# One mask product over two PSUM banks, and the old state added on the PE

## The chip, the cores and the metric

The kernel runs on 1 core of one Trainium2 chip. The metric is the device time in microseconds of a whole execution. PE is TensorE (products), PEld its weight load, DVE VectorE, ACT ScalarE, POOL GpSimd, SP SyncE, which issues most DMAs.

## The reference, cut to what matters

```
for t in range(S):                      # B=4, H=8, S=768, D=48
    state = alpha[:, :, t, :, None] * state + einsum('bhd,bhe->bhde', k[:, :, t], v[:, :, t])
    y[:, :, t] = einsum('bhd,bhde->bhe', q[:, :, t], state)
x = y as (3072 rows, 384)
# first MoE: each row goes to the one of 8 experts with the largest logit
out[mask] = gate_w[mask, None] * (maximum(x[mask] @ w1[e], 0) @ w2[e])      # F=1024
# second MoE: every row through 4 experts, weighted by domain_probs
out += p[:, e:e + 1] * (maximum(x @ w1[e], 0) @ w2[e])
```

## The kernel before, in words

`tile_main` (L40) opens the pools and calls `attention_and_routing` (L339) and `experts` (L114). Instructions run on each engine in the order in which the program writes them; a library places the semaphore waits, from the tiles that instructions read and write. Two PSUM pools serve the whole first part: `psA` with two buffers of one bank each (L98), which take turns, and `ps1` with six single ones.

**Attention, 24 units of 128 time steps.** A sequence has six units (index `u`, `c = u % 6`). The decay is folded into q and k: `prep1` (L421) makes two running products with DVE scans (`G` L434, `bf` L446), `prep2` multiplies them onto k and q, mostly on POOL (L459, L460). One unit is spread over three turns of the loop at L819:

- `S1(u)` (L473): 8 score products (L480) go alternately to two tiles `A` of `psA`, one per half of the heads, 4 x 128 columns each; two DVE products with the triangle mask `tri` (L485) bring them to SBUF as `At`, one per half. Four transposes `kn` (L492) follow.
- `S3(u)` (L554): `fin` (L558) turns the finished rows, ACT copies them out.
- `S2(u)` (L506): `y` from `At` and v (L516) and, if `c > 0`, from the old state `S` and q (L525); the new part of the state goes to the PSUM tile `U` (L537, if `c < 5`). `state()` (L543) is put at the end of the turn: on DVE, for `c = 0`, `S = U * bcall` (L547); for `c` from 1 to 4 first `U = U + S_old` (L549) and then `S = U * bcall` (L550).

Turn `i` calls `S1(i)`, `S3(i-2)`, `S2(i-1)`, so the PE does A(i), kn(i), fin(i-2), y(i-1), U(i-1), and the DVE does bf scans, At(i), routing steps, G scans, state(i-1). A(i+1) cannot start until At(i) has read the tiles `A`. Every six units a group of rows is routed, scaled and scattered by POOL (L653).

**Early rows.** The first 224 rows of the first expert window are worked while routing ends. `early_rows` (L681) transposes them into two `psA` tiles `ext`, one for two column blocks, one for the third; `cut` copies each out (ACT L675, then the remainder on DVE L676). `early_g1` (L694) makes the hidden layer for a pair of 128-blocks in one `psA` tile `eh`; `early_relu` (L707) takes it out on ACT (L710) and DVE (L711); `early_g2` (L715) adds up `eo`. The DVE part of `early_relu(0)` is written after the routing steps of the last group, behind the products of the second pair.

**First expert.** In `experts`, `xpose(0)` (L179) turns the other 224 rows in three steps (`xt` L192, ACT `xh` L197, DVE `xl` L198), each in the next `psA` tile. For each of 8 blocks `f`, `gemm1` (L132, products L135 to L137) fills a `psA` tile `h`, `h_split` (L123) takes it out on ACT (`hh` L126) and DVE (`hl` L127), and `g2(f-1)` (L224, products L233 to L235) follows, so that the products of `f` and of `f-1` alternate. At L247 these pools are closed. From the second expert on, and in the second MoE (L322), other PSUM pools are used.

Of the kernel before, what the change touches and what calls it, by code (L numbers as in the profile page):

```python
# [7 lines left out]
F32 = mybir.dt.float32  # L8
# [5 lines left out]
ALU = mybir.AluOpType  # L14
AX = mybir.AxisListType
PSUM = bass.MemoryType.PSUM

B, H, S, D = 4, 8, 768, 48
# [12 lines left out]
R = 112  # L31
# [7 lines left out]
@with_exitstack  # L39
def tile_main(ctx: ExitStack, tc: tile.TileContext, a: dict, out: bass.AP):  # L40
    nc = tc.nc

    const = ctx.enter_context(tc.tile_pool(name="const", bufs=1))
    small = ctx.enter_context(tc.tile_pool(name="small", bufs=2))
    dram = ctx.enter_context(tc.tile_pool(name="dram", bufs=1, space=bass.MemoryType.DRAM))

    xs = dram.tile([E1 * NR, DM], F32, name="xs")
    info_d = dram.tile([NT, 8], F32, name="info_d")


    units = [(0, e, f) for e in range(E1) for f in range(NFB)]
    units += [(1, e, f) for e in range(E2) for f in range(NFB)]
    wraw, wtile, ids = {}, {}, {}
    w_loaded, w_split = [0], [0]

    def load_w(n):
        while w_loaded[0] < min(n, len(units)):
            u = w_loaded[0]
            t = wst.tile([128, 2 * DM], F32, tag="wraw", name="wraw")
            src = a["wu"][u]  # L60
            if NFB <= u < E1 * NFB:
                e = a["wu"][0:E1 * NFB].rearrange("(e f) r c -> e f r c", f=NFB)
                src = e[bass.ds(ids[u // NFB], 1), u % NFB].rearrange("o r c -> (o r) c")
            nc.sync.dma_start(out=t, in_=src)
            wraw[u] = t
            w_loaded[0] += 1

    def split_w(n):
        while w_split[0] < min(n, len(units)):
            u = w_split[0]  # L70
            load_w(u + 1)
            r = wraw.pop(u)
            t = wun.tile([128, 2, 2 * DM], F32R, tag="wu", name="wu")
            nc.scalar.activation(out=t[:, 0], in_=r, func=AF.Copy)  # L74
            nc.gpsimd.tensor_tensor(out=t[:, 1], in0=r, in1=t[:, 0].bitcast(F32), op=ALU.subtract)  # L75
            wtile[u] = t
            w_split[0] += 1

    with tc.manual_schedule():
        ti = const.tile([128, 2, 128], F32, name="ti")  # L80
        ident = ti[:, 1]
        inf = const.tile([128, 24, 8], F32, name="inf")
        keep = {
            "ident": ident,
            "ti": ti,
            "ordi": const.tile([128, 8], I32, name="ordi"),
            "offi": const.tile([128, 8], I32, name="offi"),
            "posi": const.tile([128, 24], I32, name="posi"),
            "inf": inf,
            "flag": const.tile([1, 1], I32, name="flag"),  # L90
            "ft": const.tile([128, 3], F32, name="ft"),
            "ones": const.tile([128, 8], F32, name="ones"),
        }
        with ExitStack() as fast:
            wun = fast.enter_context(tc.tile_pool(name="wun", bufs=10))
            wst = fast.enter_context(tc.tile_pool(name="wst", bufs=3))
            banks = fast.enter_context(ExitStack())
            ps = (banks.enter_context(tc.tile_pool(name="psA", bufs=2, space=PSUM)),  # L98
                  banks.enter_context(tc.tile_pool(name="ps1", bufs=1, space=PSUM)))
            scat = attention_and_routing(tc, a, small, keep, xs, info_d, wst, wtile, load_w, split_w, *ps)  # L100
            experts(fast, tc, a, keep, small, xs, info_d, scat, wtile, ids, load_w, split_w, out, banks, *ps)

    bad = nc.values_load(keep["flag"][0:1, 0:1], min_val=0, max_val=1000)
    with tc.If(bad > 0):
        general(tc, a, ident, out)


def order(tc, ins, names, why):
# [230 lines left out]
def attention_and_routing(tc, a, small, keep, xs, info_d, wst, wtile, load_w, split_w, psA, ps1):  # L339
    nc = tc.nc  # L340
    ident = keep["ident"]
# [3 lines left out]
    with ExitStack() as ctx:  # L345
# [14 lines left out]
        tri = keep["ti"][:, 0]  # L360
# [4 lines left out]
        Sb = [c1.tile([R, 4, D], F32, name=f"S{j}") for j in range(2)]  # L365
# [107 lines left out]
        def S1(u):  # L473
            g, cl = divmod(u, 3)
            At = wk.tile([128, 2, 4, 128], F32, tag="At", name="At")
            ps = [psA.tile([128, 4, 128], F32, tag="A", name=f"A{h}") for h in range(2)]
            for p in range(4):
                kt, qq = (x[g, p // 2][:, 2 * cl + p % 2, :] for x in (kts, qqs))
                for h in range(2):
                    nc.tensor.matmul(  # L480
                        ps[h][:, p, :], lhsT=kt[64 * h:64 * h + D], rhs=qq[64 * h:64 * h + D],
                        start=(p == 0), stop=True, skip_group_check=True,
                    )
            for h in range(2):
                nc.vector.tensor_tensor(  # L485
                    out=At[:, h], in0=ps[h], in1=tri.unsqueeze(1).to_broadcast([128, 4, 128]), op=ALU.mult
                )
            Ats[u] = At
            if u % 6 < 5:
                pk = ps1.tile([128, 4, R], F32, tag="kn", name="kn")  # L490
                for p in range(4):
                    nc.tensor.matmul(  # L492
                        pk[:, p, :], lhsT=kts[g, p // 2][:, 2 * cl + p % 2, :], rhs=ident[0:R, 0:R],
                        is_transpose=True, start=(p == 0), stop=True, skip_group_check=True,
                    )
                kn = wk.tile([128, 4, R], F32, tag="kn", name="kn_s")
                nc.scalar.activation(out=kn, in_=pk, func=AF.Copy)
                kns[u] = kn
# [7 lines left out]
        def S2(u):  # L506
            g, cl = divmod(u, 3)
            c = u % 6
            At, v = Ats.pop(u), vins[g]
            py = ps1.tile([112, 4, 128], F32, tag="y", name="y")  # L510
            for p in range(4):
                for s in range(2):
                    o = py[0:64, p, :] if s == 0 else py[64:112, p, :]
                    c0 = p * 96 + s * 48
                    n = 64 if s == 0 else 48
                    nc.tensor.matmul(  # L516
                        o, lhsT=v[:, cl, c0:c0 + n], rhs=At[:, s, p, :],
                        start=(p == 0), stop=(c == 0), skip_group_check=True,
                    )
            if c:  # L520
                st = Sb[u % 2]
                for p in range(4):
                    qq = qqs[g, p // 2][:, 2 * cl + p % 2, :]
                    for h in (slice(0, D), slice(64, 64 + D)):
                        nc.tensor.matmul(  # L525
                            py[h, p, :], lhsT=st[h, p], rhs=qq[h], start=False, stop=True, skip_group_check=True
                        )
            yt = wk.tile([112, 4, 128], F32, tag="yt", name="yt")
            nc.scalar.activation(out=yt, in_=py, func=AF.Copy)
            yts[u] = yt  # L530
            if c < 5:
                kn = kns.pop(u)
                pu = ps1.tile([R, 4, D], F32, tag="U", name="U")
                for p in range(4):
                    for h in (slice(0, 64), slice(64, R)):
                        c0 = p * 96 + h.start // 64 * D
                        nc.tensor.matmul(  # L537
                            pu[h, p, :], lhsT=kn[:, p, h], rhs=v[:, cl, c0:c0 + D],
                            start=(p == 0), stop=True, skip_group_check=True,
                        )  # L540
                g2, cl2 = divmod(u + 1, 3)

                def state():  # L543
                    sn, so = (Sb[(u + j) % 2] for j in (1, 0))
                    bcv = bcall[:, g2, cl2].unsqueeze(2).to_broadcast([R, 4, D])
                    if c == 0:
                        nc.vector.tensor_tensor(out=sn, in0=pu, in1=bcv, op=ALU.mult)  # L547
                    else:
                        nc.vector.tensor_tensor(out=pu, in0=pu, in1=so, op=ALU.add)  # L549
                        nc.vector.tensor_tensor(out=sn, in0=pu, in1=bcv, op=ALU.mult)  # L550

                late.append(state)

# [265 lines left out]
        for i in range(NU + 5):  # L819
# [26 lines left out]
            if 0 < i < NU:  # L846
                S1(i)
# [7 lines left out]
            if 0 <= i - 1 < NU:  # L855
                S2(i - 1)
# [62 lines left out]
        def dot(out, t, x):  # L919
# [32 lines left out]
            out=pv, in0=ohb, in1=off.unsqueeze(1).to_broadcast([128, NU, 8]), op=ALU.mult  # L952
# [341 lines left out]
```

## Time and profile before

| | |
|---|---|
| three runs | 1221.97, 1223.74, 1224.63 us; median 1223.74 us |
| profiled execution | 1219.32 us, its span 1217.5 us |
| mean granted clock of the PE | 0.987 |
| busy: PE, DVE, ACT, POOL | 1177.6, 393.9, 326.5, 306.8 us |
| chain that ended last | PE 87%, DVE 4%, issue 3% |

The span runs from the first to the last instruction of the profiled execution; 1.8 us of its time lie around it. A row of the timeline gives the start, the duration, the engine, the line, out<-in, how many instructions are merged, and in brackets how long the engine had been idle and what ended that.

### The profile page before, as it was taken

What the parts mean: (1) busy time and instruction counts of PE and PEld (TensorE: products, weight loads), DVE (VectorE), ACT (ScalarE), POOL (GpSimd) and SP (SyncE); (2) the same over time, 40 slices, a digit from 0 to 9 for tenths busy, and PEclk for the clock granted to TensorE, in tenths of its full rate; (3) what the DMA queues carried; (4) which work ended last, traced back from release to release, by engine and by line L of the source; (5) the groups of instructions that cost most, each with busy time, mean ns of one, the idle gap of its engine ahead of it and who ended that gap; (6) DMA issues with size and microseconds to landing.
All of it is one profiled execution on the core that took longest, in us unless ns stands there. A gap on an engine that the chain in (4) does not pass through costs nothing.

```text
span 1217.5 us, 17436 instructions
## 1 busy us (share of the span) xinstructions
PE 1177.6 (97%) x7219; PEld 1078.6 (89%) x7219; DVE 393.9 (32%) x823; ACT 326.5 (27%) x640; POOL 306.8 (25%) x221
## 2 busy tenths in 40 slices
PE   5999979999999999999999999999999999999996
PEld 4788879999999999999999999999999999999996
DVE  8989553222222222222212222222222122222221
ACT  3466534444444311111311111221111131111111
POOL 3567543766666300000400000130000030111111
PEclk9999989999999999999999999999999999999998
DMA  9995125544443300000300000120000010000000
GB/s 236 298 278 174 54 100 172 155 141 140 133 123 121 81 1 1 1 1 1 90 15 1 1 1 1 30 75 1 1 1 1 1 40 1 27 27 26 26 27 29
DMA packets 30032, 79.98 MB, mean 66 GB/s; under 512 B 7352, under 2 KB 11064, under 8 KB 28376
## 3 DMA queue, kind: packets, MB, share of 16 engines
q1 hardware_dynamic: 26104, 69.25, 19.5%
q0 software_dynamic: 3840, 9.54, 2.2%
q8 instruction: 58, 0.95, 0.3%
q14 instruction: 30, 0.25, 0.1%
HBM read 65.21 MB, written 13.57 MB: 65 GB/s over the span
## 4 chain that ended last, share of the span: by engine, by line
PE 87%; DVE 4%; issue 3%; ACT 0%; POOL 0%; DVEq 0%; POOLq 0%; ACTq 0%
PE h L135 14%; PE h L137 13%; PE h L136 13%; PE p L303 11%; PE p L302 11%; PE p L301 10%; PE o L234 3%; PE o L235 3%; PE o L233 3%; PE fin L558 1%; PE y L516 1%; PE A L480 1%; DVE bf L446 1%; DVE G L434 1%; DVE At L485 1%
## 5 line engine op out<-in xcount | busy, mean ns | idle before, releaser
L127 DVE SCALAR_TENSOR_TENSOR hl<-h,hh 128x512 fp32r<-128x512 f32 (+9 forms) x264 | 169.9, 644 | 733.4 <-ACT hh L126 719.0
L126 ACT ACTIVATE hh<-h 128x512 fp32r<-128x512 f32 (+9 forms) x264 | 148.2, 562 | 727.1 <-PE h L137 725.3
L75 POOL TENSOR_TENSOR wu<-wraw,wu 128x768 fp32r<-128x768 f32 x96 | 176.6, 1841 | 643.9 <-ACT wu L74 643.7
L303 PE MATMUL p<-wu,hl 128*128 128x384 f32 x768 | 258.8, 337 | 0.0
L302 PE MATMUL p<-wu,hh 128*128 128x384 f32 x768 | 258.2, 336 | 0.0
L301 PE MATMUL p<-wu,hh 128*128 128x384 f32 x768 | 258.0, 336 | 0.0
L135 PE MATMUL h<-x,wu 128*128 128x512 f32 (+1 forms) x600 | 233.0, 388 | 0.0
L137 PE MATMUL h<-x,wu 128*128 128x512 f32 (+1 forms) x600 | 230.6, 384 | 0.0
L136 PE MATMUL h<-x,wu 128*128 128x512 f32 (+1 forms) x600 | 227.9, 380 | 0.0
L302 PEld LDWEIGHTS p<-wu,hh 128*128 128x128 f32 x768 | 144.3, 188 | 7.4
L301 PEld LDWEIGHTS p<-wu,hh 128*128 128x128 f32 x768 | 144.4, 188 | 7.1
L303 PEld LDWEIGHTS p<-wu,hl 128*128 128x128 f32 x768 | 144.3, 188 | 0.0
L137 PEld LDWEIGHTS h<-x,wu 128*128 128x128 f32 x600 | 112.6, 188 | 26.6
L136 PEld LDWEIGHTS h<-x,wu 128*128 128x128 f32 x600 | 112.8, 188 | 16.1
L135 PEld LDWEIGHTS h<-x,wu 128*128 128x128 f32 x600 | 112.8, 188 | 14.5
L74 ACT ACTIVATE wu<-wraw 128x768 fp32r<-128x768 f32 x96 | 80.4, 840 | 39.6 <-PE p L303 34.1
L314 POOL DMA_INDIRECT out_dram<-acc,toki x24 | 23.4, 975 | 183.4 <-DVE acc L310 178.5
L135 PE MATMUL h<-xh,wu 128*128 128x224 f32 (+7 forms) x192 | 67.4, 351 | 0.3 <-DVE xl L198 0.3
L234 PE MATMUL o<-hl,wu 128*128 128x224 f32 (+7 forms) x192 | 65.6, 341 | 0.1
L233 PE MATMUL o<-hh,wu 128*128 128x224 f32 (+7 forms) x192 | 65.6, 342 | 0.0
L136 PE MATMUL h<-xh,wu 128*128 128x224 f32 (+7 forms) x192 | 65.5, 341 | 0.0
L137 PE MATMUL h<-xl,wu 128*128 128x224 f32 (+7 forms) x192 | 65.5, 341 | 0.0
(164 smaller groups left out, 1086.2 us busy)
## 6 DMA issues: line engine op xcount, KB each, us to landing
wraw<-in_wu_dram SPq DMA_DIRECT2D x96, 384.0 KB, 3.1
tin<-in_aqk_dram SPq DMA_DIRECT2D x14, 1011.1 KB, 11.4
xw<-xs SPq DMA_DIRECT2D x7, 672.0 KB, 6.6
v<-in_v_dram SPq DMA_DIRECT2D x8, 576.0 KB, 10.3
xs<-pre SPq DMA_DIRECT2D x8, 480.0 KB, 11.0
tin<-in_aqk_dram SPq DMA_DIRECT2D x2, 448.0 KB
tin<-in_aqk_dram SPq DMA_DIRECT2D x2, 225.8 KB, 4.4
tin<-in_aqk_dram SPq DMA_DIRECT2D x2, 224.0 KB
```

What stands on the lines that cost most here:

```text
L74: nc.scalar.activation(out=t[:, 0], in_=r, func=AF.Copy)
L75: nc.gpsimd.tensor_tensor(out=t[:, 1], in0=r, in1=t[:, 0].bitcast(F32), op=ALU.subtract)
L126: nc.scalar.activation(out=hh[:, 0:n], in_=ps, func=AF.Relu)
L127: nc.vector.scalar_tensor_tensor(out=hl[:, 0:n], in0=ps, scalar=0.0, in1=hh[:, 0:n].bitcast(F32), op0=ALU.max, op1=ALU.subtract)
L135: nc.tensor.matmul(ps, lhsT=w[:, 0, ks], rhs=xh(k), start=(k == 0), stop=False)
L136: nc.tensor.matmul(ps, lhsT=w[:, 1, ks], rhs=xh(k), start=False, stop=False)
L137: nc.tensor.matmul(ps, lhsT=w[:, 0, ks], rhs=xl(k), start=False, stop=(k == KD - 1))
L233: nc.tensor.matmul(o, lhsT=w[:, 0, ds], rhs=hh[:, 0:n], start=(f == 0), stop=False)
L234: nc.tensor.matmul(o, lhsT=w[:, 0, ds], rhs=hl[:, 0:n], start=False, stop=False)
L301: nc.tensor.matmul(o, lhsT=hh[:, js], rhs=w[:, 0, DM:2 * DM], start=(f == 0), stop=False)
L302: nc.tensor.matmul(o, lhsT=hh[:, js], rhs=w[:, 1, DM:2 * DM], start=False, stop=False)
L303: nc.tensor.matmul(o, lhsT=hl[:, js], rhs=w[:, 0, DM:2 * DM], start=False, stop=(f == NFB - 1))
```

## The change

`psA` becomes one tile `A` of two banks (512 columns each), in a class `Banks` that hands out the halves in turn. `S1` writes both halves as before, and one DVE instruction over 1024 columns masks both. For `c` from 1 to 4 the PE adds the old state to `U` with a product of the identity (112 x 112) and `S` (112 x 192), and the DVE addition L549 is gone. Everything else that used `psA` (`ext`, `eh`, `xt` of the first expert, `h` of the first expert) now writes halves of the tile `A`.

```diff
-            ps = (banks.enter_context(tc.tile_pool(name="psA", bufs=2, space=PSUM)),
+            ps = (Banks(banks.enter_context(tc.tile_pool(name="psA", bufs=1, space=PSUM))),
...
+class Banks:
+    def __init__(self, pool):
+        self.both = pool.tile([128, 2, 512], F32, name="A")
+        self.n = 0
+    def tile(self, shape, *_, **__):
+        self.n += 1
+        return self.both[0:shape[0], self.n % 2, 0:shape[1]]
...
-            ps = [psA.tile([128, 4, 128], F32, tag="A", name=f"A{h}") for h in range(2)]
+            ps = psA.both.rearrange("p h (a c) -> p h a c", a=4)
...
-            for h in range(2):
-                nc.vector.tensor_tensor(
-                    out=At[:, h], in0=ps[h], in1=tri.unsqueeze(1).to_broadcast([128, 4, 128]), op=ALU.mult
-                )
+            nc.vector.tensor_tensor(
+                out=At.rearrange("p h a c -> p (h a) c"), in0=ps.rearrange("p h a c -> p (h a) c"),
+                in1=tri.unsqueeze(1).to_broadcast([128, 8, 128]), op=ALU.mult,
+            )
...
+                if c:
+                    nc.tensor.matmul(
+                        pu, lhsT=ident[0:R, 0:R], rhs=Sb[u % 2], start=False, stop=True, skip_group_check=True
+                    )
...
-                    sn, so = (Sb[(u + j) % 2] for j in (1, 0))
-                    if c == 0:
-                        nc.vector.tensor_tensor(out=sn, in0=pu, in1=bcv, op=ALU.mult)
-                    else:
-                        nc.vector.tensor_tensor(out=pu, in0=pu, in1=so, op=ALU.add)
-                        nc.vector.tensor_tensor(out=sn, in0=pu, in1=bcv, op=ALU.mult)
+                    nc.vector.tensor_tensor(out=Sb[(u + 1) % 2], in0=pu, in1=bcv, op=ALU.mult)
```

In `S1` and `state()` no instruction changes its place; at three places the waits of the PE change (lines of the changed kernel are 11 or 12 higher, and what wrote `ext`, `eh` and `h` now writes `A`). The first is the PE in `early_rows` and the products after it, `rkb` being sums for the routing; before, and then now:

```order
736 L686 MATMUL ext<-ti,exw 128x112 [waits DMAHW4_49]
737 L686 MATMUL ext<-ti,exw 128x112 x5
738 L592 LDWEIGHTS trib
739 L592 MATMUL rkb<-ohb,trib 128x16 [waits DVE_49]
740 L592 LDWEIGHTS oneb
```

```order
626 L697 MATMUL A<-ti,exw 128x112 [waits DMAHW4_49]
627 L697 MATMUL A<-ti,exw 128x112 x3
628 L697 MATMUL A<-ti,exw 128x112 [waits DVE_49]
629 L697 MATMUL A<-ti,exw 128x112
630 L603 LDWEIGHTS trib
631 L603 MATMUL rkb<-ohb,trib 128x16
```

The six transposes ran on in one row; now the last two, which fill the second tile `ext`, come after a wait for the DVE, that is, for `cut` of the first. The second place is the PE at the second pair of `early_g1` and the first `early_g2`, before and then now:

```order
751 L702 MATMUL eh<-ext,wu 128x224 x9
752 L702 MATMUL eh<-ext,wu 128x224 [waits PE_49]
753 L702 MATMUL eh<-ext,wu 128x224 x17
754 L724 MATMUL eo<-eh,wu 128x224 [waits Activation_49]
755 L724 MATMUL eo<-eh,wu 128x224 [waits DVE_49]
756 L724 MATMUL eo<-eh,wu 128x224 x4
```

```order
641 L713 MATMUL A<-ext,wu 128x224 x11
642 L713 MATMUL A<-ext,wu 128x224 [waits Activation_49]
643 L713 MATMUL A<-ext,wu 128x224 x17
644 L735 MATMUL eo<-eh,wu 128x224 [waits PE_49]
645 L735 MATMUL eo<-eh,wu 128x224 [waits DVE_49]
646 L735 MATMUL eo<-eh,wu 128x224 x4
```

The second pair (row 642) now starts after ACT has taken the first pair out. The third place is the PE in the first expert, at the end of `gemm1(1)` and the start of `g2(0)` before:

```order
810 L137 MATMUL h<-xl,wu 128x224
811 L233 MATMUL o_2546<-hh,wu 128x224 [waits Activation_49]
812 L234 MATMUL o_2546<-hl,wu 128x224 [waits DVE_49]
813 L235 MATMUL o_2546<-hh,wu 128x224
814 L233 MATMUL o_2547<-hh,wu 128x224
```

Now, from the start of `g2(0)`'s last product group to the start of `gemm1(2)`:

```order
704 L247 MATMUL o_2465<-hh,wu 128x224
705 L245 MATMUL o_2466<-hh,wu 128x224
706 L246 MATMUL o_2466<-hl,wu 128x224
707 L247 MATMUL o_2466<-hh,wu 128x224
708 L147 MATMUL A<-xh,wu 128x224 [waits DVE_49]
```

The wait for the DVE has left `g2` (row 812) and stands at the first product of `gemm1` (row 708, which had no wait before): there, and before `gemm1(1)` too, the PE waits until `hl` of the block before is out of the other half. In the same way the second and the third `xt` now wait for the DVE to finish `xl` of the one before, and `gemm1(0)` waits for the last `xl`.

## Rows read from the trace of the kernel before

**Rows 1.** The page, part 1: busy time, share of the span, instructions.
```profile
PE 1177.6 (97%) x7219; PEld 1078.6 (89%) x7219; DVE 393.9 (32%) x823; ACT 326.5 (27%) x640; POOL 306.8 (25%) x221
```
**Rows 2.** Stretches: us, busy of PE, PEld, DVE, ACT, POOL, granted clock, DMA, GB/s.
```profile
24.00:57.00 33.00, 30.59 (x361) 26.23 (x362) 30.55 (x64) 15.40 (x45) 17.10 (x16) 1.00 0.98 290
...
62.00:84.70 22.70, 22.15 (x332) 19.31 (x328) 20.80 (x55) 15.02 (x39) 12.03 (x9) 0.99 0.89 262
...
131.00:152.00 21.00, 21.00 (x318) 18.85 (x316) 12.81 (x45) 13.36 (x34) 7.60 (x7) 1.00 0.12 44
...
210.00:1217.00 1007.00, 996.34 (x5181) 918.46 (x5179) 239.06 (x393) 226.84 (x378) 200.13 (x131) 1.00 0.14 41
```
**Rows 3.** Timeline of the DVE, one turn of the attention loop.
```profile
43.79 1.26 DVE L485 TENSOR_TENSOR At<-A,ti 128x512 f32<-128x512 f32 x2
...
46.88 0.34 DVE L549 TENSOR_TENSOR U<-U,S 112x192 f32<-112x192 f32 x1
47.26 0.36 DVE L550 TENSOR_TENSOR S<-U,bcall 112x192 f32<-112x192 f32 x1
...
49.95 1.26 DVE L485 TENSOR_TENSOR At<-A,ti 128x512 f32<-128x512 f32 x2
```
**Rows 4.** Timeline of the PE in the attention loop.
```profile
79.31 1.75 PE L480 MATMUL A<-bf,G 48*128 48x128 f32 x16 [0.44 <-DVE At L485]
...
115.01 1.75 PE L480 MATMUL A<-bf,G 48*128 48x128 f32 x16 [0.71 <-DVE At L485]
...
140.48 1.16 PE L480 MATMUL A<-bf,G 48*128 48x128 f32 x16
...
142.01 1.05 PE L558 MATMUL fin<-cst,yt 112*128 112x104 f32 x8
142.99 1.09 PE L516 MATMUL y<-At,v 128*64 128x128 f32 x16
144.01 1.08 PE L525 MATMUL y<-bf,S 48*48 48x128 f32 x16
...
145.62 1.16 PE L480 MATMUL A<-bf,G 48*128 48x128 f32 x16
```
**Rows 5.** A stretch of the loop at a lower clock, columns as in rows 2.
```profile
115.00:120.00 5.00, 4.88 (x40) 4.29 (x40) 4.79 (x13) 4.12 (x10) 2.35 (x3) 0.71 0.13 47
```
**Rows 6.** Timeline of PE, ACT and DVE, early rows.
```profile
167.76 0.74 PE L686 MATMUL ext<-ti,exw 112*128 112x112 f32 x6
...
169.75 0.92 DVE L676 TENSOR_TENSOR ext<-ext 128x448 fp32r<-128x448 f32 x2
...
170.43 5.91 PE L702 MATMUL eh<-ext,wu 128*128 128x224 f32 x36 [0.22 <-DVE ext L676]
...
173.58 0.55 ACT L710 ACTIVATE eh<-eh 128x448 fp32r<-128x448 f32 x1 [3.62 <-PE eh L702]
...
175.84 0.61 DVE L711 SCALAR_TENSOR_TENSOR eh<-eh 128x448 fp32r<-128x448 f32 x1
...
176.17 2.50 PE L724 MATMUL eo<-eh,wu 128*128 128x224 f32 x18
...
178.55 2.25 PE L702 MATMUL eh<-ext,wu 128*128 128x224 f32 x18
```
**Rows 7.** Timeline of all engines, start of the first expert.
```profile
188.68 0.55 PE L192 MATMUL xt<-ti,xw 112*128 112x112 f32 x4
...
189.91 0.41 PE L192 MATMUL xt<-ti,xw 112*128 112x112 f32 x2 [0.68 <-DVE xl L198]
190.20 0.37 PE L135 MATMUL h<-xh,wu 128*128 128x224 f32 x1
...
194.90 0.28 PE L233 MATMUL o<-hh,wu 128*128 128x224 f32 x1
...
195.49 0.39 DVE L127 SCALAR_TENSOR_TENSOR hl<-h,hh 128x224 fp32r<-128x224 f32 x1 [2.10 <-ACT hh L126]
...
195.91 0.27 PE L135 MATMUL h<-xh,wu 128*128 128x224 f32 x1
```

More of the change, by code (lines that the diff above doesn't have):

```diff
@@ L480, in S1 @@
                     nc.tensor.matmul(
-                        ps[h][:, p, :], lhsT=kt[64 * h:64 * h + D], rhs=qq[64 * h:64 * h + D],
+                        ps[:, h, p, :], lhsT=kt[64 * h:64 * h + D], rhs=qq[64 * h:64 * h + D],
                         start=(p == 0), stop=True, skip_group_check=True,
                     )
-            for h in range(2):
-                nc.vector.tensor_tensor(
-                    out=At[:, h], in0=ps[h], in1=tri.unsqueeze(1).to_broadcast([128, 4, 128]), op=ALU.mult
-                )
+            nc.vector.tensor_tensor(
+                out=At.rearrange("p h a c -> p (h a) c"), in0=ps.rearrange("p h a c -> p (h a) c"),
+                in1=tri.unsqueeze(1).to_broadcast([128, 8, 128]), op=ALU.mult,
+            )
             Ats[u] = At
```

## The prediction

> **What bounds the kernel now.** The page's busy shares come first [rows 1]: PE 97%, DVE 32%. That mean hides stages, so the stretches come next [rows 2]. From 24 to 57 us of the attention part the DVE is busy for 30.55 of 33.00 us and the PE for 30.59; from 62 to 84.7 us they stand at 20.80 and 22.15 of 22.70; from 131 to 152 us the PE is busy for all of 21.00 and the DVE for 12.81. From 210 us to the end the PE is busy for 996 of 1007 us. Two things follow. An instruction taken from the DVE is worth something only early in the attention part, and one added to the PE costs its full length from 131 us on; and a delay before 210 us stays to the end, because no later idle time can take it up.
>
> The timeline of the DVE shows a turn where it sets the pace: one pair of mask products begins 6.16 us after the other (43.79 to 49.95) [rows 3]. The timeline of the PE shows a turn where it does: `A` begins 5.14 us after `A` (140.48 to 145.62) [rows 4].
>
> **The attention part.** One mask product replaces two in 24 units. The pair takes 1.26 us [rows 3]; one instruction of 1024 columns saves at most a start. By its nearest rows, the pair and twice the single 0.34 us for 192 columns, I take 0.06 us saved, between 0 and 0.1. The At chain has no new wait in it: `A` of the next unit already waited for both halves, since its eight products alternate between them. At 79.31 us `A` starts after the first half but takes 1.75 us instead of 1.16, that is, it stands 0.59 us until the second half is out [rows 4].
>
> The addition L549 is gone in 16 units. With its gap it holds the DVE for 0.38 us (46.88 to 47.26) [rows 3]. So a DVE turn shrinks by 0.38 + 0.06 = 0.44 us where the DVE sets the pace.
>
> The identity product (112 x 112 by 112 x 192, float32) is not in the trace. Four `fin` products of 104 columns take 0.98 us (142.01 to 142.99), 0.245 each, by columns 0.45 for 192. Eight `y` products in four pairs of 128 columns take 1.02 us (142.99 to 144.01), 0.255 a pair, by columns 0.38 [rows 4]. I take 0.38, the wider row being the nearer; the ends are 0.30 (part of a product's time being its start) and 0.45. Sixteen are 16 x 0.38 = 6.1 us of PE work, which the DVE turn covers in part:
>
> - 24 to 57 us: the PE has room (30.59 of 33.00). Four units with `c > 0` gain 0.44 each: -1.8 us.
> - 62 to 84.7 us: the PE stands only 0.44 + 0.59 = 1.03 us, all before the `A` at 79.31 [rows 4]; three identity products take 1.14 of it. The PE becomes the bound: 0. The same from 94 to 116 us.
> - 131 to 152 us: the PE has no room; four units cost 0.38 each: +1.5 us.
>
> That is -0.3 us. It could be better: from 115 to 120 us the mean granted clock is 0.71, between the levels of 2.4 and 1.2 GHz [rows 5], right behind 0.71 us of idle time and the long `A` at 115.01 [rows 4]; a second such stretch stands around 60 us. 5.00 us at 0.71 lose 1.45. If a busier PE avoids both, the part gains 2.9 us more.
>
> **The waits that the change adds.** The order of the changed kernel shows them: the two halves belong to one tile, so whoever writes one half waits for the last reader of the other. In the attention part that costs nothing, as said. In the early rows and the first expert the halves stood for two tiles that took turns.
>
> Early rows [rows 6]. The last two transposes now wait for the DVE's first `cut`, which before ended just before the PE's start at 170.43 us; then ACT, the DVE again, and only then `early_g1(0)`. The same cycle (transposes, ACT, DVE, next transposes) is seen in the first expert, 188.68 to 189.91 = 1.23 us [rows 7]: +1.23. The second pair of `early_g1` now waits for ACT's `early_relu(0)`, 0.55 us, with about 0.1 for the handing over: +0.65. The DVE part of that relu is written after the second pair and now waits for it, so `early_g2(0)` starts 0.61 + 0.1 us after the pair; before, that relu started at 175.84 and ended at 176.45, 0.28 after `g2` began at 176.17: +0.43. What is queued behind it, `early_relu(1)` on ACT, is out 1.2 us later, inside the 2.4 us of `early_g2(0)` (176.17 to 178.55), and delays nothing. Sum +2.3 us, between 1.5 and 3.5.
>
> First expert [rows 7]. Before, the second tile `xt` started at once and the third 1.23 us after the first; `gemm1(0)` began 1.52 us after the first transposes (188.68 to 190.20). Now three cycles of 1.23 us stand in front: 3.69, so +2.17. `gemm1(1)` must wait for `hl(0)`: a `gemm1` that ends at 194.90 has its `hl` out at 195.49 + 0.39 = 195.88, about 1.0 us. `g2(0)` had such a wait before, so part of this was paid; I take +0.4, between 0 and 1.0. For the six blocks after that the wait runs beside `g2`, which takes 194.90 to 195.91 = 1.01 us, as long as the wait: +0.03 each, +0.2. Sum +2.8 us, between 2.2 and 3.8.
>
> **Sum.** -0.3 + 2.3 + 2.8 = +4.8 us against the profiled execution's own 1219.32 us: 1224.1. That execution lies 4.4 us below the median of the three runs, so I put the same 4.8 us onto the median: 1228.5 us.
>
> **A rule against the trace.** At 195.91 us `gemm1` starts without a wait, with `hl` out of the other tile just before, at 195.88 [rows 7]; the order of the changed kernel makes its first product wait for that `hl`. The Trainium skill's Perfetto Trace Analysis, Optimizing Tensor Performance (Matmuls), says that independent groups of products should rotate through PSUM banks so that taking out one overlaps the products of the next. The halves do lie in two banks, so by that rule alone 5.1 us of waits would be nothing and the sum would be -0.3 us; here the waits are in the program's order, so I do not follow it, and it is rival 2's ground. The same page, Optimizing Scalar/DVE Operations, says that where Scalar or Vector are not saturated but cause bubbles elsewhere, breaking an instruction up may let work be completed sooner; the change does the reverse. By it `A` would start 0.6 us later; the row at 79.31 has `A` end with the second half anyway, so no term changes.
>
> **Rivals.**
> 1. The PE avoids the stretches at the lower clock. For: they follow idle time of the PE, of which 6.1 us of extra work removes some. Against: DMA and the long stops there stay. Price: 4.8 - 2.9 = +1.9: 1225.6 us.
> 2. Faster: the waits cost next to nothing, since the other reader has mostly finished when the wait comes, and the attention part gains what the DVE is relieved of. It decides if the waits cost under 1 us and both clock stretches go: -0.3 - 2.9 = -3.2, and with 0.5 for the waits -2.7: 1221.0 us. Against it: the chain of three cycles is serial by its order.
> 3. The new idle times between 168 and 195 us let the granted clock fall as idle times do in the loop. One stretch as in [rows 5] costs 1.45 us, and two 2.9: +7.7: 1231.4 us.
> 4. The change does not do what it says: the wide product takes as long as two and the identity product 0.45 us. Then the first stretch gains 1.5 and 131 to 152 us loses 1.8, the middle ones lose 0.3 each: +0.9 instead of -0.3: 1229.7 us.
>
> **How the numbers follow.** A measurement of this kernel can tell about 0.2% from no change, 2.45 us: 1221.3 to 1226.2. The forecast, with rival 4 close beside it, has 0.54, rival 1 has 0.18, rival 2 has 0.10, rival 3 has 0.18. Faster by more than that is rival 2: 0.10. The same is rival 1 and a small part of the forecast: 0.20. Slower is the rest: 0.70. The forecast's own range, by the bounds of the waits (3.7 to 7.3) and the attention part (-1.0 to +0.9), is 1226.4 to 1231.9. The range reaches up to it and rival 3, 1232.5, and down past rival 1 to 1222.5, leaving rival 2 out.
>
> **What would show it.** Right: sixteen rows of an identity product of about 0.38 us on the PE; 24 mask products of 1024 columns of about 1.2 us; a DVE turn of 5.7 us around 45 us; a PE turn of 5.5 us around 141 us; idle time of the PE before the third block's transposes, the second pair and the first expert's `xt` and first two blocks, ended by the DVE or ACT; the stretch from 210 us as long as before. Wrong: the first expert's `gemm1(0)` starting less than 2 us after its first transposes, or a first expert that starts earlier than before by more than 1 us, which would put the attention part off.

## The result, and the profile after

The changed kernel takes 1236.86 us (median of 14 runs, 1229.65 to 1241.23), the kernel before 1224.16 us (14 runs, 1220.72 to 1228.10). The ratio is 1.0097, 95% interval 1.0081 to 1.0113: 11.9 us slower by the ratio (the medians lie 12.7 us apart), where 4.8 us were forecast and 1232.5 us was the top of the range. The direction held, the size did not.

The profiled execution took 1236.45 us, span 1234.7. That of before, 1219.32 us, is nearly the fastest of its kernel; so the 17.1 us between the two profiles is more than the change costs, and stages are compared below over several profiles. By the trace, 8.1 of the 17.1 us lie ahead of the early rows (their first transposes start at 175.83 us instead of 167.76), 3.2 in the early rows and 5.7 in the first expert.

The page, part 1, of the changed kernel:

```profile
PE 1188.7 (96%) x7251; PEld 1085.5 (88%) x7251; DVE 388.5 (31%) x783; ACT 326.3 (26%) x640; POOL 306.9 (25%) x221
```

The DVE has 40 instructions less than before [rows 1] and 5.4 us less work: 24 for the merged masks and 16 additions. The PE has 32 rows more, two for each identity product. Its stretches follow. The first three are at the same times as in [rows 2], though not at the same instructions. The fourth is the first expert from its first transposes to those of the next expert, which the program puts behind `gemm1` of the fourth of the eight blocks; this stretch is called the first expert below. The last is the rest:

```profile
24.00:57.00 33.00, 31.30 (x389) 26.60 (x390) 30.14 (x56) 16.06 (x46) 18.41 (x17) 1.00 0.97 289
62.00:84.70 22.70, 20.82 (x249) 17.39 (x249) 16.89 (x42) 11.24 (x33) 10.23 (x7) 0.85 0.93 277
131.00:152.00 21.00, 21.00 (x267) 18.51 (x267) 11.19 (x31) 11.84 (x31) 11.86 (x8) 0.88 0.15 48
199.92:214.87 14.95, 11.45 (x71) 10.50 (x70) 3.73 (x10) 3.37 (x10) 1.80 (x1) 0.77 0.39 117
215.00:1222.00 1007.00, 1006.72 (x5272) 928.77 (x5271) 242.02 (x401) 233.04 (x391) 203.74 (x132) 1.00 0.14 41
```

From 215 us on the PE is busy for 1006.72 of 1007 us: nothing there takes up a delay, as forecast. (The 996.34 us of [rows 2] include some 10.7 us behind the last product. From the next expert's transposes to the end of the last product it is 1008.4 us before and 1008.7 us now, by the trace.) The same first expert in the kernel before, from 188.68 to 197.91 us [rows 7]:

```profile
188.68:197.91 9.23, 8.40 (x71) 7.88 (x70) 3.54 (x10) 3.15 (x10) 1.84 (x2) 1.00 0.69 207
```

The same 71 products (by the trace) take 14.95 us instead of 9.23, with the PE busy for 11.45 instead of 8.40 at a mean granted clock of 0.77 instead of 1.00. So only part of the 5.72 us is waiting; the PE is also busy longer with the same work. The timeline of the PE there shows where:

```profile
199.92 0.36 PE L204 MATMUL A<-ti,xw 112*128 112x112 f32 x2
201.15 0.41 PE L204 MATMUL A<-ti,xw 112*128 112x112 f32 x2 [0.87 <-DVE xl L210]
202.44 0.41 PE L204 MATMUL A<-ti,xw 112*128 112x112 f32 x2 [0.88 <-DVE xl L210]
203.72 0.37 PE L147 MATMUL A<-xh,wu 128*128 128x224 f32 x1 [0.87 <-DVE xl L210]
...
205.06 0.41 PE L149 MATMUL A<-xl,wu 128*128 128x224 f32 x1
206.35 0.55 PE L147 MATMUL A<-xh,wu 128*128 128x224 f32 x1 [0.87 <-DVE hl L139]
...
208.62 0.41 PE L246 MATMUL o<-hl,wu 128*128 128x224 f32 x1
...
211.50 0.27 PE L148 MATMUL A<-xh,wu 128*128 128x224 f32 x1
```

Four waits of 0.87 us, at the four places that the order of the changed kernel showed. `gemm1(0)` starts 3.80 us after the first transposes (199.92 to 203.72; forecast 3.69). But from about 204.4 to 211 us a row is 0.41 us long where before and after that it is 0.27. The mean granted clock is 0.50 from 204.7 to 210.9 us by the trace: the lower level, 1.2 GHz.

### The profile page after: what moved, and what is told of

The parts are those of the page before. It is cut to its first block, busy times and chain, and to the rows that moved or that the text cites. A ratio compares the mean times of both kernels' runs of the same rounds, so it can differ in the third digit from the quotient of the medians.

```text
span 1234.7 us, 17471 instructions
## 1 busy us (share of the span) xinstructions
PE 1188.7 (96%) x7251; PEld 1085.5 (88%) x7251; DVE 388.5 (31%) x783; ACT 326.3 (26%) x640; POOL 306.9 (25%) x221
## 4 chain that ended last, share of the span: by engine, by line
PE 89%; issue 3%; DVE 3%; DMA 2%; SPq 1%; ACT 1%; POOL 0%; POOLq 0%; DVEq 0%; ACTq 0%
PE h L147 13%; PE h L149 13%; PE h L148 13%; PE p L315 10%; PE p L314 10%; PE p L313 10%; PE o L246 3%; PE o L245 3%; PE o L247 3%; PE y L528 2%; PE A L492 1%; PE fin L569 1%; DMA tin<-in_aqk_dram 1%; PE y L537 1%; DMA wraw<-in_wu_dram 1%
## 5 line engine op out<-in xcount | busy, mean ns | idle before, releaser
L139 DVE SCALAR_TENSOR_TENSOR hl<-h,hh 128x512 fp32r<-128x512 f32 (+8 forms) x256 | 166.9, 652 | 725.8 <-ACT hh L138 715.5
L138 ACT ACTIVATE hh<-h 128x512 fp32r<-128x512 f32 (+8 forms) x256 | 145.4, 568 | 719.4 <-PE h L149 717.6
L74 ACT ACTIVATE wu<-wraw 128x768 fp32r<-128x768 f32 x96 | 80.4, 840 | 47.8 <-PE p L315 34.3
L245 PE MATMUL o<-hh,wu 128*128 128x224 f32 (+7 forms) x192 | 66.0, 344 | 0.0
L247 PE MATMUL o<-hh,wu 128*128 128x224 f32 (+7 forms) x192 | 65.8, 343 | 0.0
L147 PE MATMUL h<-xh,wu 128*128 128x448 f32 (+6 forms) x168 | 60.6, 360 | 0.3 <-DVE xl L210 0.3
L148 PE MATMUL h<-xh,wu 128*128 128x448 f32 (+6 forms) x168 | 58.9, 350 | 0.0
```

The lines of the kernel that those rows point to most:

```text
L138: nc.scalar.activation(out=hh[:, 0:n], in_=ps, func=AF.Relu)
L139: nc.vector.scalar_tensor_tensor(out=hl[:, 0:n], in0=ps, scalar=0.0, in1=hh[:, 0:n].bitcast(F32), op0=ALU.max, op1=ALU.subtract)
L147: nc.tensor.matmul(ps, lhsT=w[:, 0, ks], rhs=xh(k), start=(k == 0), stop=False)
L148: nc.tensor.matmul(ps, lhsT=w[:, 1, ks], rhs=xh(k), start=False, stop=False)
L245: nc.tensor.matmul(o, lhsT=w[:, 0, ds], rhs=hh[:, 0:n], start=(f == 0), stop=False)
L247: nc.tensor.matmul(o, lhsT=w[:, 1, ds], rhs=hh[:, 0:n], start=False, stop=(f == NFB - 1))
```

## The experiments

"Before" in each line is the kernel before, run beside it. The batches ran on several chips, on some of which the kernel before takes 1225 us and on others 1212 us; so ratios are compared, and twice the pair was run on one chip. Line numbers in the profiles of the experiments differ by a few.

**1. The change without the sharing.** The two-bank tile serves the attention part alone; then its pool is closed and two tiles of one bank are opened. Shown is the method that hands out the tiles:

```diff
     def tile(self, shape, dt, tag, name):
+        if self.pool is None:
+            self.one.close()
+            self.pool = self.stack.enter_context(self.tc.tile_pool(name="psB", bufs=2, space=PSUM))
+        return self.pool.tile(shape, dt, tag=tag, name=name)
...
-        self.n += 1
-        return self.both[0:shape[0], self.n % 2, 0:shape[1]]
```

> The change with its shared tile kept for the attention part alone: the early rows and the first expert write two tiles of one bank again. Theory W (the waits between the two halves, and the lower clock that their idle times bring, make most of the loss): about 1228 us, +4 on the kernel before, the stage from the early transposes to the end of the first expert as long as before. Theory I (the identity product and what it does to the attention part makes most of the loss): about 1233 us.

Measured: ratio 1.0016 (0.9995 to 1.0038), 2.0 us. Most of the loss is gone with the sharing.

**2. The sharing alone.** Two mask products on the halves of the shared tile, the addition on the DVE as before.

```diff
-                    nc.tensor.matmul(
-                        pu, lhsT=ident[0:R, 0:R], rhs=Sb[u % 2], start=False, stop=True, skip_group_check=True
-                    )
...
+                        nc.vector.tensor_tensor(out=pu, in0=pu, in1=so, op=ALU.add)
...
+            for h in range(2):
+                nc.vector.tensor_tensor(
+                    out=At[:, h], in0=ps[:, h], in1=tri.unsqueeze(1).to_broadcast([128, 4, 128]), op=ALU.mult
+                )
```

> The kernel before with the one two-bank tile alone, shared by all users: two mask products of one half each, the addition by the DVE. Nothing is taken from any engine; only waits between the halves are added. Theory W: +6 to +9 us, all behind 165 us. Theory I: +3 us or less.

Measured: 1.0067 (1.0043 to 1.0091), 8.2 us, though nothing was added to any engine. With experiment 1 this is theory W. The first expert in its profile, and in that of experiment 1:

```profile
196.56:211.50 14.94, 11.45 (x71) 10.50 (x70) 3.72 (x10) 3.35 (x10) 1.26 (x1) 0.77 0.37 114
```

```profile
198.21:207.62 9.41, 8.40 (x72) 7.89 (x70) 3.54 (x10) 3.71 (x11) 3.55 (x2) 1.00 0.65 201
```

**3. The identity product alone, and the one mask product alone,** each with separate tiles of one bank behind the attention part. The edits are those of the change's diff, one at a time; with the identity product alone the attention part has its two tiles and two mask products as before.

> The kernel before with the identity product alone (two mask products, two tiles of one bank). Theory I: +6 us or more, the first scores of the last unit 6 us later. Theory W: +1 to +3 us.

> The one mask product alone: the two-bank tile for the attention part, two tiles of one bank after it, the old state added by the DVE as before. Both theories: within 1.5 us of the kernel before, if anything below it.

Measured: identity product 1.0009 (0.9986 to 1.0031), mask product 1.0012 (0.9994 to 1.0030). Neither can be told from no change.

**4. The sharing in one stage only.** The shared tile serves the attention part and either the early rows or the first expert (attention as in experiment 2). The line shown is that of the early rows, beside experiment 1's.

```diff
     def tile(self, shape, dt, tag, name):
-        if self.pool is None:
+        if name in ("xt0", "h") and self.pool is None:
...
```

> The kernel before with the shared tile for the attention part and the early rows alone (two mask products, addition on the DVE), two tiles of one bank from the first expert on. Early transposes to the first expert's transposes 2.3 to 3.2 us longer than before, first expert as before, total +2.3 to +3.5 us.

> The kernel before with the shared tile for the attention part and the first expert alone, two tiles of one bank for the early rows. First expert (its first transposes to those of the next) 5.7 us longer than before, early rows as before, total +5 to +6 us; with the run of the early rows' sharing the two add up to the 8 us of both.

Measured: early rows 1.0026 (1.0005 to 1.0048), 3.2 us; first expert 1.0043 (1.0024 to 1.0063), 5.2 us on this chip. The sum, 8.4, is about that of experiment 2, 8.2; each has some 2.5 us of uncertainty. For the first expert the profiles agree more sharply than the times. The PE's time from the first transposes of the early rows to those of the first expert, and from those to the first of the next expert, in us:

```
                      sharing in       early rows   first expert
before                none               20.92          9.23
experiment 1          none               20.12          9.41
identity product      none               20.12          9.53
mask product          none               22.04          9.23
first expert only     first expert       20.66         14.96
early rows only       early rows         24.26          9.24
experiment 2          both               23.65         14.94
changed kernel        both               24.09         14.95
```

With the sharing the early rows take 24.0 us in the mean instead of 20.8, +3.2, and the first expert 14.95 instead of 9.33, +5.6. The first expert's +5.6 stands clear of the spread. The early rows' rests mainly on the pair of this experiment, 24.26 and 20.66 us on one chip, for the stage can be as long without sharing: three profiles of experiment 8 (both products, the identity product alone and the kernel before, each with later weight splits, on one chip) have 22.99, 23.42 and 24.01 us there, behind a wait of the PE for the routing of 2.53 to 3.26 us. The longest of these:

```profile
161.39 0.17 PE L592 MATMUL rkb<-ohb,trib 128*128 128x16 bf16 x1 [3.26 <-DVE ohb L1012]
```

**5. The waits filled with idle work.** Is the second half of the first expert's loss the clock? In the changed kernel the PE gets seven products that nobody reads in each of the four waits.

```diff
+        def dummy():
+            for n in range(7):
+                nc.tensor.matmul(
+                    dum[:, 0:224], lhsT=wtile[7][:, 0, 0:128], rhs=wtile[7][:, 0, 0:224],
+                    start=True, stop=True, skip_group_check=True,
+                )
...
+                if e == 0:
+                    dummy()
...
+                if (e, f) == (0, 0):
+                    dummy()
```

> The changed kernel with 28 idle products (seven of 128x128 by 128x224 after each of the three transposes and after the first gemm1, into a free bank, read by nobody) that run inside the PE's four waits of 0.87 us at the start of the first expert. Theory C (behind those waits the granted clock falls and that costs as much again as the waits): the clock stays up, the first expert is 3.3 us shorter, the time about 3 us below the changed kernel, though work is added. Theory W (the loss is the waits alone): no change, or up to 0.5 us slower.

Measured: 1.0054 (1.0029 to 1.0078), against 1.0097 of the changed kernel; and, with both on one chip:

> The changed kernel beside the next three on one chip. All theories: 1.0097 times the kernel before if this does not depend on the chip; 1.007 to 1.008 if the attention part loses less on a chip on which the PE's stops of 4 us are missing.

> The idle products in the first expert's four waits, beside the changed kernel on the same chip. Theory C: 2.6 us below the changed kernel (14.95 us of first expert against 12.32). Theory W: as the changed kernel.

Measured there: changed kernel 1.0112 (1.0085 to 1.0138), with idle products 1.0063 (1.0040 to 1.0087): 6.0 us less. The first expert in the profile of the first of these runs:

```profile
189.43:201.75 12.32, 11.97 (x99) 11.13 (x98) 3.73 (x10) 3.37 (x11) 1.83 (x1) 1.00 0.45 136
```

```profile
189.43 0.36 PE L213 MATMUL A<-ti,xw 112*128 112x112 f32 x2
...
193.23 0.37 PE L147 MATMUL A<-xh,wu 128*128 128x224 f32 x1
```

28 products more, the clock stays at 1.00, and the stage is 2.63 us shorter (14.95 to 12.32). The serial start is as long as ever: `gemm1(0)` starts 3.80 us after the first transposes (189.43 to 193.23), so the gain lies behind it. So of the 5.6 us, 3.0 are waits and 2.6 the lower clock behind them. The times show more than 2.6, some 5 and 6 us, but with some 4 us of uncertainty each, so that anything beyond the stage's 2.6 is not shown.

**6. The transposes out of the shared tile.** `xt` of the first expert in three banks that are free there; `h` stays shared.

```diff
-            "xt": lambda e, k: psA.tile([128, W0], F32, tag="A", name="xt0") if e == 0
+            "xt": lambda e, k: ps1.tile([128, W0], F32, tag=("dcon", "y", "U")[k], name="xt0") if e == 0
```

> The changed kernel with the three transposes of the first expert in three banks of their own, the halves staying shared in the attention part, the early rows and for h. Theory W: gemm1(0) starts some 1.5 us after the first transposes again, the wait before gemm1(1) stays, 2.3 us less. Theory C: 2.3 us and also 3.3 us of the lower clock less, 5.6 in all, if one wait of 0.87 us alone does not bring the clock down.

Measured: 1.0024 (1.0004 to 1.0044), on the chip of experiment 4. The PE in its first expert:

```profile
183.94 0.74 PE L204 MATMUL xt<-ti,xw 112*128 112x112 f32 x6
184.75 0.37 PE L147 MATMUL A<-xh,wu 128*128 128x224 f32 x1
...
187.48 0.37 PE L147 MATMUL A<-xh,wu 128*128 128x224 f32 x1 [1.26 <-DVE hl L139]
187.69 0.27 PE L148 MATMUL A<-xh,wu 128*128 128x224 f32 x1
...
188.14 0.41 PE L149 MATMUL A<-xl,wu 128*128 128x224 f32 x1
```

`gemm1(0)` starts 0.81 us after the transposes. The one wait left, 1.26 us long, is again followed by rows of 0.41 us. The stage takes 11.42 us, 3.5 less than the changed kernel's and 2.1 more than without sharing, at a mean granted clock of 0.85 by the trace. Neither theory's figure came out: one wait was enough here, though it is longer than the 0.87 us of theory C's "if", which stays untested. A longer wait need not bring the clock down: in experiment 8's identity product with later splits the PE waits once for 1.69 us in the same stage, which keeps a granted clock of 1.00 (10.23 us, PE busy for 8.39, by the trace):

```profile
181.21 0.41 PE L192 MATMUL xt<-ti,xw 112*128 112x112 f32 x2 [1.69 <-DVE xl L198]
```

What makes the difference is open. So is the time: by the ratios this version is 8.8 us below the changed kernel, 5 us more than the stage gives; the changed kernel was not run on this chip.

**7. The changed kernel again, without the identity product, and with two.** All on one chip.

> The changed kernel once more, for a second profile on the chip of the two runs beside it. Both theories: about 1.0097 times the kernel before; four waits of the PE of about 0.87 us at the start of the first expert, and half the granted clock behind them for some 6 us.

> The changed kernel without the identity product: one mask product, one shared tile for all users, the addition on the DVE again. Theory W with C: it loses what the sharing alone lost, +8 us (1.0067). Theory I: half of the changed kernel's loss or less, +6 us at most.

> The changed kernel with two tiles of one bank after the attention part, and each identity product issued twice: first into U ahead of the products of the new part, which overwrite it, then as in the change. It adds 16 times 0.51 = 8.2 us to the PE. If the PE sets the pace of nearly all of the attention part, +7 to +8 us on the run without the sharing (+9 to +10 on the kernel before); if the DVE, the DMA or the stops set it for half of the turns, +4.

Measured: again 1.0089 (1.0058 to 1.0119); without the identity product 1.0056 (1.0032 to 1.0079); with the product twice and no sharing 1.0066 (1.0040 to 1.0092), 8.1 us, which is 6.1 above experiment 1 for 8.2 us of added work, with some 4 us of uncertainty. By these figures a second identity product costs three quarters of its length, while the first costs nothing that shows in experiment 3. That the 0.38 us which the DVE no longer needs pay for the first is an argument, not shown by a run. The changed kernel without the product (1.0056) lies below the changed kernel (1.0089), but the intervals overlap; whether the product costs something there is open.

**8. The weights split later.** Why is the loop no faster, when the DVE turn is shorter? ACT's eight weight splits (`wu`, L74) are issued two turns later.

```diff
-            if 6 <= i < 22 and i % 2 == 0:
-                split_w((i - 4) // 2)
+            if 8 <= i < 24 and i % 2 == 0:
+                split_w((i - 6) // 2)
```

> The kernel before with each of ACT's eight weight splits in the attention part issued two turns later; nothing else. Theory L (the loop runs into the landing of the weights, where ACT waits with the PE's next operands queued behind it): ACT's two waits there, 1.2 and 2.0 us, go, the time is 0 to 2 us less. Theory P (the PE and the stops set the attention part): no change.

> The kernel before with the identity product and the later splits. Theory L: the gain of the relieved DVE, which the wait of 6.9 us took back, stays: 2 to 4 us under the identity product alone, and under the kernel before with later splits too. Theory P: as the identity product alone.

> The one mask product and the identity product with separate tiles after the attention part, and the later splits: the best version if theory L holds, 2 to 4 us below the kernel before. Theory P: as without the later splits, +2 us.

> The identity product alone, beside the next on the same chip. Theory L: ACT waits for a weight load for over 5 us, and the time is within 2 us of the kernel before. Theory P: the same time as the next.

> The identity product with the later weight splits. Theory L: 2 to 4 us below the identity product alone. Theory P: no change.

Measured: the kernel before with later splits 0.9996 (0.9980 to 1.0011); the identity product with them 0.9981 (0.9962 to 1.0000); both products with them 0.9990 (0.9970 to 1.0010). On one chip: identity product alone 1.0016 (0.9995 to 1.0036), with later splits 0.9996 (0.9976 to 1.0017). ACT and PE of the identity product alone (last pair):

```profile
72.69 0.84 ACT L74 ACTIVATE wu<-wraw 128x768 fp32r<-128x768 f32 x1 [6.73 <-DMA wraw<-in_wu_dram]
73.54 0.52 ACT L497 ACTIVATE kn_s<-kn 128x448 f32<-128x448 f32 x1
```

```profile
72.00 1.16 PE L480 MATMUL A<-bf,G 48*128 48x128 f32 x16
74.12 0.60 PE L492 MATMUL kn<-ti,G 112*128 112x112 f32 x4 [0.95 <-ACT kn_s L497]
...
79.74 1.16 PE L480 MATMUL A<-bf,G 48*128 48x128 f32 x16
```

And with the later splits:

```profile
71.58 1.16 PE L480 MATMUL A<-bf,G 48*128 48x128 f32 x16
...
77.22 1.16 PE L480 MATMUL A<-bf,G 48*128 48x128 f32 x16
```

The turn that held ACT's wait takes 5.64 us with the later splits instead of 7.74. (The two waits of the PE in that turn, 0.95 us and one of 0.82 before `fin`, were not followed by a lower clock: it is 1.00 by the trace.) The times go the same way by 2.4 us, and by 3.4 us across chips, but the intervals overlap: that the loop gains time by it is not shown. None of these versions beats the kernel before by more than its uncertainty; the best, 0.9981, has an interval that ends at 1.0000. All of them lie below the changed kernel.

## Why the prediction was wrong

The change cost 7.1 us more than forecast. By stage, 2.8 of that lie in the first expert, 0.9 in the early rows and 2.3 in the attention part, where the interval is wider than that; 1.1 us are not placed.

**First expert: the step that failed.** The forecast put +2.8 us there, all of it waits. As waits it was right: 3.0 us by experiment 5, and `gemm1(0)` at 3.80 us. What failed is that the fall of the granted clock was put at nothing in the sum and left to rival 3 with a chance of 0.18 and a stretch or two of 1.45 us somewhere. It came in all six profiles that have the shared first expert with its four waits left empty, always behind these waits, and cost 2.6 us. The Trainium skill's Perfetto Trace Analysis, Matmul Optimizations, says that the engine scales power by utilization, so products should run back to back; the run with idle products agrees, with 12.32 us for 99 products at a granted clock of 1.00 against 14.95 us for 71 at 0.77.

**Early rows: right mechanism, somewhat too small.** Forecast +2.3 (1.5 to 3.5), measured +3.2 in the profiles, with the spread told in experiment 4, and 3.2 us (0.6 to 5.8) in the time. The three waits are there, as the timeline of the changed kernel shows:

```profile
175.83 0.55 PE L697 MATMUL A<-ti,exw 112*128 112x112 f32 x4
178.51 0.64 PE L697 MATMUL A<-ti,exw 112*128 112x112 f32 x2 [2.13 <-DVE ext L687]
...
180.02 4.07 PE L713 MATMUL A<-ext,wu 128*128 128x224 f32 x18 [0.59 <-DVE ext L687]
184.77 2.27 PE L713 MATMUL A<-ext,wu 128*128 128x224 f32 x18 [0.68 <-ACT eh L721]
...
187.76 2.15 PE L735 MATMUL eo<-eh,wu 128*128 128x224 f32 x17 [0.60 <-DVE eh L722]
```

The first products start 4.19 us after the first transposes instead of 2.67 [rows 6], +1.52 for a forecast 1.23; 0.68 before the second pair (forecast 0.65); 0.60 before `early_g2(0)` (forecast 0.43 added). That third wait is not shown to be added: in experiment 1, without sharing, it is 0.90 us by the trace. The 18 products of the first pair take 4.07 us, at a granted clock of 0.52 by the trace, and those of the second 2.27, so here too a part is the clock; before, the two pairs together took 5.91 us, so some of it was lost already, and in experiment 1 4.28 us at 1.00.

**The halves belong to one tile: right.** Experiments 1, 2 and 4 show that sharing makes 8.2 of the 11.9 us (5.3 to 11.1), and that the two stages named account for it within the intervals. The 2.0 us of experiment 1 make 10.2 with it; the remaining 1.7 lies inside the intervals. The two halves are two banks, and the PE waited all the same, because the program makes it wait for the tile. The rule of the Trainium skill's Perfetto Trace Analysis, Optimizing Tensor Performance (Matmuls), that groups of products should rotate through PSUM banks, did not save it, as the prediction argued. Rival 2, waits that cost next to nothing, is out.

**The DVE: right.** A merged mask product takes 1.20 us (0.06 less), and the turn 5.69 us (forecast 5.7):

```profile
42.77 1.20 DVE L496 TENSOR_TENSOR At<-A,ti 128x1024 f32<-128x1024 f32 x1
...
48.46 1.20 DVE L496 TENSOR_TENSOR At<-A,ti 128x1024 f32<-128x1024 f32 x1
```

**The identity product: undersized.** It takes 0.51 us (44.31 to 44.82), above the forecast's 0.38 and its upper end of 0.45, and a PE turn 5.64 us where 5.5 was forecast:

```profile
44.31 0.58 PE L554 MATMUL U<-S,ti 112*112 112x192 f32 x2
44.82 1.16 PE L492 MATMUL A<-bf,G 48*128 48x128 f32 x16
...
146.67 1.16 PE L492 MATMUL A<-bf,G 48*128 48x128 f32 x16
...
152.31 1.16 PE L492 MATMUL A<-bf,G 48*128 48x128 f32 x16
```

It is 0.13 us too small sixteen times, 2.1 us of PE work. The nearest row was the `fin` product, by columns 0.45, not the paired `y` products.

**The attention part: -0.3 forecast, +2.0 measured (the time of experiment 1), with an interval of -0.6 to +4.7.** The forecast lies inside it, so this term is not shown to be wrong, only its identity product. The profiles cannot settle it: the early rows begin 8.1 us later than in the profile of before, but in experiment 2 and with the mask product alone, both without the identity product, they also begin at 172.91 and 175.63 us instead of 167.76. In the changed kernel's profile the loop was faster at first, as forecast: four turns take 21.88 us (`A` at 33.53 to `A` at 55.41) instead of 23.74 (33.08 to 56.82), 1.9 less for a forecast 1.8. Then it lost this, and more, in a turn that holds waits which the prediction did not name:

```profile
72.34 0.84 ACT L74 ACTIVATE wu<-wraw 128x768 fp32r<-128x768 f32 x1 [6.83 <-DMA wraw<-in_wu_dram]
73.19 0.52 ACT L509 ACTIVATE kn_s<-kn 128x448 f32<-128x448 f32 x1
...
74.53 0.62 ACT L541 ACTIVATE yt<-y 112x512 f32<-112x512 f32 x1
```

```profile
71.55 1.16 PE L492 MATMUL A<-bf,G 48*128 48x128 f32 x16
73.77 0.60 PE L504 MATMUL kn<-ti,G 112*128 112x112 f32 x4 [1.05 <-ACT kn_s L509]
75.20 2.03 PE L569 MATMUL fin<-cst,yt 112*128 112x104 f32 x8 [0.82 <-ACT yt L541]
...
82.25 1.16 PE L492 MATMUL A<-bf,G 48*128 48x128 f32 x16
```

ACT stands 6.83 us for a weight load; `kn_s` and `yt` are queued behind it, the PE waits for them for 1.05 and 0.82 us, and then its rows are twice as long (`fin` 2.03 us, 1.05 in [rows 4]; granted clock 0.50 from 75 to 79 us, by the trace): one turn of 10.70 us. Experiment 8 takes the wait away and the long turn goes. Why the wait is so long is only in part known. By the traces it is 1.97 us in the kernel before and up to 2.40 in experiment 4, 4.70 in experiment 2, 5.61 with the mask product alone and 6.38 to 7.88 wherever the identity product runs with the splits in their old place. Experiment 2 takes nothing from the DVE, so a faster loop is not the only source.

Rival 1, a PE that avoids the lower clock, came by halves. The two stretches that it named are at a granted clock of 1.00 in this profile (55.4 to 71.5 us and 120 to 125 us, by the trace), but the long turn is a new one: from 62 to 84.7 us the clock fell to 0.85 from 0.99 [rows 2].

## What to carry to other kernels

When buffers are merged into one tile, list every user of the old ones and read the waits at each: a merge that helps one loop can make neighbours serial. Waits of about a microsecond on the PE can have two prices, their length and the rows behind them at the lower clock. The second is not sure (a wait of 1.69 us came without it, four of 0.87 us brought it every time), so read it from the same kind of gap elsewhere in the trace and give it a term in the sum. And before counting a faster loop as gain, look for what it may then wait for: here a load whose consumer stood ahead of the loop's own work on ACT.

## What had not been expected of the hardware

Adding work can save time: with 28 products that nobody reads, put into the PE's waits, the first expert was 2.63 us shorter, and the granted clock stayed at 1.00 where it had been 0.77. And a single wait of 1.26 us was followed by rows of 0.41 us instead of 0.27 within 0.7 us of its end, while one of 1.69 us in the same stage of another run was not.
